# Block-decayed attention ahead of a mixture of experts: attention in blocks of 64 tokens instead of chunks of 128

## The chip, the cores and the metric

The kernel runs on one core of a Trainium2 chip. Of its engines, TensorE (PE in the profile) multiplies matrices: a weight load (PEld) puts up to 128 x 128 numbers into its array, then a matmul streams the other operand through it. A float32 matmul runs as two passes, so each appears twice in the counts. The array can be used in parts: a profile row that says 64\*64 worked on a quarter of it, 64\*128 on half of its rows, 128\*64 on half of its columns. VectorE (DVE), ScalarE (ACT) and GpSimd (POOL) work on tiles of 128 partitions; matmul results land in PSUM banks of 128 partitions x 512 floats. Sixteen DMA engines move data, started here almost only from SyncE's queue (SPq).

The metric is the device time of one execution in microseconds (us), the median of several.

## The reference

Attention over 4 batches, 8 heads, 768 tokens and 64 dimensions per head, in blocks of 64 tokens, with a decay `lam` per head; its output becomes `x`, 3072 tokens by 512, of a mixture of four experts.

```python
for b in range(nb):                                    # 12 blocks of 64 tokens
    qb, kb, vb = (q[:, :, sl], k[:, :, sl], v[:, :, sl])
    intra = np.einsum('bhic,bhjc->bhij', qb, kb) * Dmask[None]      # lam ** (i - j) for i >= j
    intra = np.einsum('bhij,bhjd->bhid', intra, vb)
    inter = np.einsum('bhid,bhde->bhie', qb * lam_pow[None], kv_state)   # lam ** (i + 1)
    out[:, :, sl] = intra + inter
    kb_dec = kb * rev_pow[None]                        # lam ** (63 - j)
    kv_state = lam_block * kv_state + np.einsum('bhsd,bhse->bhde', kb_dec, vb)   # lam ** 64
...
p = domain_probs / (domain_probs.sum(-1, keepdims=True) + 1e-09)
for e in range(4):
    h = np.maximum(x @ w1[e], 0.0)                     # 3072x512 by 512x1024
    out += p[:, e:e + 1] * (h @ w2[e])                 # 3072x1024 by 1024x512
```

Everything is float32. The block length isn't part of the result: any chunk length gives the same sums, with decays to match.

## The kernel before, in words

**Tiles.** Attention goes in 24 chunks of C = 128 tokens (6 of each batch, NCH), each with all 8 heads. Eight chunks (CPG) make a group of 1024 tokens, whose attention output, transposed, is `xT`, the operand of that group's expert products. There are three groups (g) and four experts (e). The expert products are Strassen products: seven half-size products M1 to M7 for x @ w1, each split into seven again (`first_product`, line 843, operands `xs_in` and `ws_in` prepared in DRAM and brought in by `feed`, two buffers each), and seven for h @ w2 (`second_product`, line 897, operand `w2t`). The last group uses a nested form for the second (line 1123), the first unit a direct form (line 1253).

**A chunk of attention** has three steps. Heads are kept in pairs: partitions 0 to 63 of `qT` and `kT` hold heads 0 to 3, partitions 64 to 127 heads 4 to 7 (`half[r]`).

- `turn` (line 520) transposes q and k on TensorE (line 529), copies them out of PSUM on ScalarE, scales q by its decays on VectorE (`qs`), and has GpSimd scale k in place by its decays (`decayed`). For chunks 2 to 5 of batches 2 and 3 q and k come rearranged through DRAM instead (`across`), and VectorE transposes them in 32 x 32 squares.
- `scores` (line 543) multiplies k by q for the whole chunk: per head 128 keys by 128 queries over 64 dimensions, 8 matmuls on half of the array's rows (line 551). VectorE multiplies them with the mask of decays, two operations of 512 elements (`mask`, line 95), into the tiles `st`.
- `values` (line 563) sums in the same PSUM banks the product with the state `kv` (line 574, 8 matmuls on quarters of the array, left out in a batch's first chunk) and that of `st` with v (line 579, 8 matmuls on half of its columns). In the second bank's free half it computes the products of decayed k and v for the state (line 587, 8 matmuls; left out in a batch's last chunk). ScalarE copies the sums to `xT`. VectorE then scales the state by lam ** 128 and adds the products (line 95; in a batch's first chunk a copy, line 599).

**Order.** The schedule is manual: each engine runs its instructions in the order in which the program issues them, and an instruction waits for its operands with everything behind it. Group 0's attention is a loop of ten slots: slot i holds turn(i), scores(i - 1), values(i - 2), in slot 3 scores ahead of turn; direct products stand between them from slot 4 on. Groups 1 and 2 have their attention as a list of 24 `steps` each, one or two of which are popped per Strassen product, so chunks 8 to 23 stand among the products of the group before. VectorE's share of such a step isn't issued at once: `soon` puts it at the head of a list, `background`, of which `rest` issues one entry per part of a product; for chunks 0 to 7 it is issued at once. Sums for the operands (GpSimd) and their stores are `chores`, which `pump` issues at a pace, from an account of GpSimd's work (`busy`).

q, k and v of chunks 0 to 3 are loaded ahead of the loop in the order q k of 0, q k of 1, v of 0, q k of 2, v of 1, q k of 3, a weight block, v of 2, v of 3; later chunks some slots ahead. Small tiles of 128 x 512 come from one pool of NPOOL = 47 buffers that is handed round in order.

**Tables.** `s_decay` (the mask, 8 scans over 128 elements) and `q_decay` (powers of lam by seven doublings) are computed on VectorE at the start, once `lam` has arrived; chunk 0's masks come behind them.

Of the kernel before, what the change touches and what calls it, by code (L numbers as in the profile page):

```python
# [14 lines left out]
FP32 = mybir.dt.float32  # L15
PSUM = bass.MemoryType.PSUM
DRAM = bass.MemoryType.DRAM
NPOOL = 47
AHEAD = 2


# [1 line left out]
def kernel(  # L23
# [30 lines left out]
    nc = tc.nc  # L54
# [3 lines left out]
    NTOK, DOUT = out.shape  # L58
    P = nc.NUM_PARTITIONS
    C = P  # L60
    NHP = H // 2
    NCH = S // C
    CPG = 8
# [76 lines left out]
    def store(f):  # L140
        queue.append((busy[0] + 2, f))

    def pump(pace=1.0, force=False):
        while results:
            results.pop(0)()
        while late and (force or late[0][0] <= now[0]):
            late.pop(0)[1]()
        begins = chores and (force or free[0] <= now[0])
        while queue and (force or queue[0][0] <= now[0] or begins and len(queue) > LEFT):
            queue.pop(0)[1]()  # L150
        if begins:
# [266 lines left out]

    s_decay = consts.tile([P, 2, NHP, C], FP32, name="s_decay")
    for r in range(2):
        for ac in range(NHP):
            h = 4 * r + ac
            nc.vector.tensor_tensor_scan(
                out=s_decay[:, r, ac], data0=lam_bc[:, h:h + 1].to_broadcast([P, C]), data1=ident[:],
                initial=0.0, op0=ALU.mult, op1=ALU.add,
            )

    k_decay = s_decay[:, :, :, C - 1]  # L430


    q_decay = consts.tile([P, NHP, C], FP32, name="q_decay")
    for r in range(2):
        nc.vector.tensor_copy(out=q_decay[half[r], :, 0], in_=lam_bc[half[r], 4 * r:4 * r + 4])
    m = 1
    while m < C:
        nc.vector.tensor_tensor(
            out=q_decay[:, :, m:2 * m], in0=q_decay[:, :, 0:m],
            in1=q_decay[:, :, m - 1:m].to_broadcast([P, NHP, m]), op=ALU.mult,  # L440
        )
        m *= 2

    kv = consts.tile([P, NHP, D], FP32, name="kv")

    probs = consts.tile([P, NTOK // P, E], FP32, name="probs")
    gate = consts.tile([P, NTOK // P, E], FP32, name="gate")
# [49 lines left out]
        if n < CPG:  # L497
            rest(len(work))

    def decayed(kn):  # L500

        kd = kn.rearrange("p (ac r) d -> p ac r d", r=2)
        by = k_decay.rearrange("p r ac -> p ac r").unsqueeze(3)
        tt(nc.gpsimd, kd, kd, by.to_broadcast([P, NHP, 2, D]), ALU.mult)

    def turn_across(n):

        qT, kT, kn = nat.pop((n, "qx")), nat.pop((n, "kx")), nat[n, "k"]
        qs = small("qs") if n % NCH else None

        def scaled():
            if n % NCH:
                tt(nc.vector, qs[:], qT[:], q_decay[:].rearrange("p h c -> p (h c)"), ALU.mult)
            turned[n] = qT, kT, qs

        soon(n, *(lambda x=x: nc.vector.transpose(out=x[:], in_=x[:]) for x in (qT, kT)), scaled)
        if n % NCH < NCH - 1:
            decayed(kn)

    def turn(n, tags):  # L520
        if comes_across(n):
            turn_across(n)
            return
        qn, kn = nat.pop((n, "q")), nat[n, "k"]
        qp = bank(tags[0], "qp")
        kp = bank(tags[1], "kp")
        for x, y in ((qp, qn), (kp, kn)):
            for ac in range(NHP):
# [4 lines left out]
        qT, kT, qs = small("qT"), small("kT"), None  # L533
        nc.scalar.copy(out=qT[:], in_=qp[:])
        nc.scalar.copy(out=kT[:], in_=kp[:])
        if n % NCH:
            qs = small("qs")
            soon(n, lambda: tt(nc.vector, qs[:], qT[:], q_decay[:].rearrange("p h c -> p (h c)"), ALU.mult))
        turned[n] = qT, kT, qs
        if n % NCH < NCH - 1:  # L540
            decayed(kn)

    def scores(n, tags):
        while n not in turned:
            rest(force=True)
        qT, kT, _ = turned[n]

        sp = [bank(tags[r], "sp") for r in range(2)]
        for ac in range(NHP):
            for r in range(2):  # L550
                nc.tensor.matmul(  # L551
                    out=sp[r][:, ac * C:(ac + 1) * C], lhsT=hc(kT)[half[r], ac], rhs=hc(qT)[half[r], ac],
                    start=True, stop=True,
                )
        st = [small("st") for _ in range(2)]

        def mask(hd):
            tt(nc.vector, st[hd][:], sp[hd][:], s_decay[:, hd].rearrange("p h c -> p (h c)"), ALU.mult)

        soon(n, *(lambda hd=hd: mask(hd) for hd in range(2)))  # L560
        masked[n] = st

    def values(n, tags):
        kn, vn = nat.pop((n, "k")), nat.pop((n, "v"))
        qs = turned.pop(n)[2]
        st = masked.pop(n)
        c = n % CPG
        first, last = n % NCH == 0, n % NCH == NCH - 1

        op = [bank(tags[r], "op") for r in range(2)]  # L570
        heads = [(a, r, c) for a in range(2) for r in range(2) for c in range(2)]
        if not first:
            for a, r, x in heads:
                nc.tensor.matmul(  # L574
                    out=op[r][half[x], a * C:(a + 1) * C], lhsT=kv[half[r], 2 * a + x], rhs=hc(qs)[half[r], 2 * a + x],
                    start=(a == 0), stop=False, skip_group_check=True,
                )
        for a, r, x in heads:
            nc.tensor.matmul(  # L579
                out=op[r][half[x], a * C:(a + 1) * C], lhsT=vn[:, 4 * r + 2 * a + x], rhs=hc(st[r])[:, 2 * a + x],  # L580
                start=(first and a == 0), stop=True, skip_group_check=True,
            )
        kvp = op[1][:, 2 * C:].rearrange("p (h d) -> p h d", d=D)
        if not last:
            for ac in range(NHP):
                for r in range(2):
                    nc.tensor.matmul(  # L587
                        out=kvp[half[r], ac], lhsT=kn[:, 2 * ac + r], rhs=vn[:, 4 * r + ac], start=(ac == 0), stop=True,
                        skip_group_check=True,
                    )  # L590
        for r in range(2):
            nc.scalar.copy(
                out=xT[:, 2 * r:2 * r + 2, c * C:(c + 1) * C],
                in_=op[r][:, 0:2 * C].rearrange("p (a t) -> p a t", t=C),
            )
        if not last:
            def state():
                if first:
                    nc.vector.tensor_copy(out=kv[:], in_=kvp)
                else:  # L600
                    tt(nc.vector, kv[:], kv[:], q_decay[:, :, C - 1:C].to_broadcast([P, NHP, D]), ALU.mult)
                    tt(nc.vector, kv[:], kv[:], kvp, ALU.add)

            soon(n, state)

    def attention(g):

# [2 lines left out]
        for n in range(g * CPG, (g + 1) * CPG):  # L610
# [3 lines left out]
            def end(n=n):  # L614
# [3 lines left out]
                values(n, ("s0", "s1"))  # L618
                if n + AHEAD < B * NCH:
                    load_more(n + AHEAD)  # L620
                if n == g * CPG + CPG // 2 - 1:
                    chores[0:0] = early
                if n == g * CPG + CPG - 1:
# [894 lines left out]
```

## Time and profile before

The median of three runs is 1185.82 us (1185.27 to 1186.21). One execution was profiled; its span, from the first to the last instruction, is 1183.3 us.

Busy time of the engines in four stretches, with the number of instructions; DMA is the mean busy share of the 16 DMA engines, the clock the granted TensorE clock as a share of full speed:

| us | what runs | PE busy | PE passes | DVE busy | ACT busy | POOL busy | clock | DMA |
|---|---|---|---|---|---|---|---|---|
| 0 to 57 | chunks 0 to 7, first direct products | 54.80 | 635 | 38.24 | 20.67 | 26.50 | 1.00 | 0.86 |
| 57 to 134 | direct products | 76.37 | 357 | 53.52 | 18.72 | 43.58 | 1.00 | 0.87 |
| 134 to 668 | products of groups 0 and 1, chunks 8 to 23 among them | 533.60 | 3192 | 359.85 | 94.54 | 247.29 | 1.00 | 0.93 |
| 668 to 1183.3 | products of the rest, no attention | 510.99 | 2380 | 339.05 | 140.08 | 311.36 | 1.00 | 0.72 |

Rows of attention, over the whole run:

| line, operands | what | passes or operations | median ns of one |
|---|---|---|---|
| 529 qp, kp | transposes of q and k (full array, 128 columns) | 128 | 273 |
| 551 sp<-qT,kT and the brought-across qx,kx | scores (half the rows, 128 columns) | 384 | 272 |
| 574 op<-qs,kv | with the state (quarters, 128 columns) | 320 | 269 |
| 579 op<-st,vn | with the values (half the columns, 128 columns) | 384 | 273 |
| 587 op<-vn,kn | products for the state (half the columns, 64 columns) | 320 | 222 |
| 95 st<-sp,s_decay (DVE) | masks, 128 x 512 | 48 | 680 |
| 95 kv<-op (DVE) | sum of the state, 128 x 256 | 16 | 421 |
| 95 kn<-kn,s_decay (POOL) | decays of k, 128 x 512 | 20 | 1060 |

The nanoseconds of one pass are its time from start to end. Passes follow each other before the one ahead has ended, so a row's time is not its count times this.

### The profile page before, as it was taken

What the parts mean: (1) busy time and instruction counts of PE and PEld (TensorE: products, weight loads), DVE (VectorE), ACT (ScalarE), POOL (GpSimd) and SP (SyncE); (2) the same over time, 40 slices, a digit from 0 to 9 for tenths busy, and PEclk for the clock granted to TensorE, in tenths of its full rate; (3) what the DMA queues carried; (4) which work ended last, traced back from release to release, by engine and by line L of the source; (5) the groups of instructions that cost most, each with busy time, mean ns of one, the idle gap of its engine ahead of it and who ended that gap; (6) DMA issues with size and microseconds to landing.
All of it is one profiled execution on the core that took longest, in us unless ns stands there. A gap on an engine that the chain in (4) does not pass through costs nothing.

```text
span 1183.3 us, 17880 instructions
## 1 busy us (share of the span) xinstructions
PE 1175.7 (99%) x6559; PEld 1022.7 (86%) x6559; DVE 790.7 (67%) x1333; ACT 274.0 (23%) x500; POOL 628.7 (53%) x600
## 2 busy tenths in 40 slices
PE   9999999999999999999999999999999999999998
PEld 8888888888888888888888888888888888888887
DVE  6785785567468857647856774773665676777785
ACT  3332122112211201211220120121243342341331
POOL 2756258349457900055244655416584693783884
PEclk9999999999999999999999999999999999999999
DMA  9797799999999997899998989998986657566543
GB/s 232 194 292 238 250 300 310 362 326 333 353 359 334 328 291 227 262 287 303 303 317 247 295 287 318 275 312 294 316 289 238 261 196 272 212 237 248 213 155 95
DMA packets 265608, 324.23 MB, mean 274 GB/s; under 512 B 121489, under 2 KB 206897, under 8 KB 265521
## 3 DMA queue, kind: packets, MB, share of 16 engines
q1 hardware_dynamic: 254912, 320.27, 81.6%
q10 hardware_dynamic: 10608, 2.82, 1.1%
q8 instruction: 52, 0.85, 0.3%
q14 instruction: 36, 0.29, 0.1%
HBM read 237.69 MB, written 89.54 MB: 277 GB/s over the span
## 4 chain that ended last, share of the span: by engine, by line
PE 94%; DVE 3%; DMA 2%; issue 0%; POOL 0%; SPq 0%; ACT 0%; DVEq 0%
PE pg L843 38%; PE q L897 32%; PE pq L1123 13%; PE pM L1253 2%; PE op L579 2%; PE sp L551 2%; PE pc L1253 2%; DMA w_ops<-ops 2%; PE op L574 1%; PE op L587 1%; DVE sums L95 0%; PE qp L529 0%; PE kp L529 0%; PE pg L1123 0%; DVE acc L95 0%; DVE m L95 0%
## 5 line engine op out<-in xcount | busy, mean ns | idle before, releaser
L843 PE MATMUL pg<-xs_in,ws_in 128*128 128x256 f32 x1960 | 469.8, 380 | 0.9 <-DVE m L95 0.9
L843 PEld LDWEIGHTS pg<-xs_in,ws_in 128*128 128x128 f32 x1960 | 371.2, 190 | 52.9 <-DVE m L95 2.3
L95 DVE TENSOR_TENSOR m<-pg,m 128x512 f32<-128x512 f32 x451 | 308.1, 687 | 106.5 <-PE pg L843 99.6
L897 PE MATMUL q<-w2t,hS 128*128 128x256 f32 x1024 | 243.4, 380 | 0.0
L897 PEld LDWEIGHTS q<-w2t,hS 128*128 128x128 f32 x1024 | 193.2, 190 | 27.0 <-issue 0.2
L913 DVE SCALAR_TENSOR_TENSOR acc<-q,gate,acc 128x256 f32<-128x256 f32 x192 | 92.5, 482 | 170.2 <-PE q L897 170.0
L897 PE MATMUL q<-w2t,m 128*128 128x256 f32 x768 | 182.7, 381 | 0.0
L897 PEld LDWEIGHTS q<-w2t,m 128*128 128x128 f32 x768 | 144.8, 190 | 20.5 <-issue 0.3
L855 ACT ACTIVATE m<-m 128x512 f32<-128x512 f32 x132 | 83.0, 630 | 283.6 <-DVE m L95 276.6
L95 POOL TENSOR_TENSOR m<-m,xT 128x512 f32<-128x512 f32 x64 | 80.7, 1276 | 71.6 <-ACT m L855 53.9
L95 POOL TENSOR_TENSOR kn<-kn,s_decay 128x512 f32<-128x512 f32 x20 | 22.5, 1126 | 140.7 <-PE kp L529 134.8
L95 DVE TENSOR_TENSOR sums<-pq,sums 128x256 f32<-128x256 f32 x153 | 64.2, 422 | 46.0 <-PE pq L1123 38.8
L851 ACT COPY m<-pg 128x512 f32<-128x512 f32 x88 | 51.6, 586 | 174.3 <-PE pg L843 173.4
L1123 PE MATMUL pq<-acc,w2t 128*128 128x256 f32 x352 | 86.6, 379 | 0.0
L95 POOL TENSOR_TENSOR ops<-w2b 128x256 f32<-128x256 f32 x24 | 17.9, 766 | 119.4 <-DMA w2b<-in_moe_w_dram 111.3
L1123 PEld LDWEIGHTS pq<-acc,w2t 128*128 128x128 f32 x352 | 66.8, 190 | 9.3 <-issue 0.3
L95 POOL TENSOR_TENSOR acc<-hT,hT 128x512 f32<-128x512 f32 x32 | 40.3, 1274 | 30.3 <-PE pq L1123 28.4
L95 POOL TENSOR_TENSOR w2o<-w2b 128x512 f32<-128x512 f32 x32 | 40.6, 1291 | 23.3 <-DMA w2b<-in_moe_w_dram 23.3
L786 ACT ACTIVATE m<-m 128x512 f32<-128x512 f32 x44 | 27.7, 630 | 101.8 <-DVE m L95 101.8
L95 DVE TENSOR_TENSOR hS<-m,m 128x512 f32<-128x512 f32 x56 | 45.3, 812 | 4.9 <-ACT m L855 4.9
L95 DVE TENSOR_TENSOR m<-m,m 128x512 f32<-128x512 f32 x56 | 47.2, 844 | 0.0
L95 POOL TENSOR_TENSOR acc<-hT,acc 128x512 f32<-128x512 f32 x32 | 40.7, 1273 | 7.4 <-PE pq L1123 5.4
(158 smaller groups left out, 1360.4 us busy)
## 6 DMA issues: line engine op xcount, KB each, us to landing
xs_in<-x_ops SPq DMA_DIRECT2D x70, 896.0 KB, 6.4
ws_in<-w_ops SPq DMA_DIRECT2D x70, 896.0 KB, 8.7
w2t<-w_ops SPq DMA_DIRECT2D x66, 256.0 KB, 6.8
w2t<-w_sums SPq DMA_DIRECT2D x64, 256.0 KB, 3.9
w_ops<-ops SPq DMA_DIRECT2D x28, 512.0 KB, 5.5
w2t<-in_moe_w_dram SPq DMA_DIRECT2D x48, 256.0 KB, 3.4
w2b<-in_moe_w_dram SPq DMA_DIRECT2D x32, 256.0 KB, 5.9
w_sums<-w2o SPq DMA_DIRECT2D x16, 512.0 KB, 5.1
```

The source lines that it names most:

```text
L95: eng.tensor_tensor(out=o, in0=a, in1=b, op=op)
L551: nc.tensor.matmul(out=sp[r][:, ac * C:(ac + 1) * C], lhsT=hc(kT)[half[r], ac], rhs=hc(qT)[half[r], ac], start=True, stop=True,)
L574: nc.tensor.matmul(out=op[r][half[x], a * C:(a + 1) * C], lhsT=kv[half[r], 2 * a + x], rhs=hc(qs)[half[r], 2 * a + x], start=(a == 0), sto ...
L579: nc.tensor.matmul(out=op[r][half[x], a * C:(a + 1) * C], lhsT=vn[:, 4 * r + 2 * a + x], rhs=hc(st[r])[:, 2 * a + x], start=(first and a = ...
L786: nc.scalar.activation(out=o[:], in_=o[:], func=AF.Relu)
L843: nc.tensor.matmul(out=p[:, j * 256:(j + 1) * 256], lhsT=ws[i][:, j * P:(j + 1) * P], rhs=xs[i], start=(fresh and j == 0), stop=True, skip ...
L851: nc.scalar.copy(out=new[at][:], in_=p[:])
L855: nc.scalar.activation(out=new[at][:], in_=new[at][:], func=AF.Relu)
L897: nc.tensor.matmul(out=p[:, s * DH:(s + 1) * DH], lhsT=h[A_OF[m]][:, c * 256 + s * P:c * 256 + (s + 1) * P], rhs=fed2[g, e, m][uu][:, c], ...
L913: nc.vector.scalar_tensor_tensor(out=o, in0=x, scalar=w, in1=o, op0=ALU.mult, op1=ALU.add)
L1123: nc.tensor.matmul(out=p[:, 0:256], lhsT=fed3[e, m, x // 2][:, x % 2, c * P:(c + 1) * P], rhs=b[B_OF[i]][:, c * 256:(c + 1) * 256], start= ...
L1253: nc.tensor.matmul(out=p[:, s * 256:(s + 1) * 256], lhsT=a[c][:, f:f + P], rhs=b[:, c, j * 256:(j + 1) * 256], start=(s == 0 and c == 0 an ...
```

## The change

Attention keeps its 24 chunks of 128 tokens and their steps, but treats each as two blocks of BL = 64 tokens (index x).

- `scores` multiplies keys and queries of the same block only: 16 matmuls of 64 x 64 by 64 columns, each on a quarter of the array (row half r, the heads; column half x, the block). The scores of both head halves fill 256 columns of a bank each, so the masks are two operations of 256 elements into one tile `st`.
- The products for the state move from `values` to `scores`, one set per block (16 matmuls of 64 x 64; 8 in a batch's last chunk), into the other 256 columns of the two banks. They read the decayed k, which is now a tile of its own (`kd`), made in `turn` for every chunk, and v.
- There are two states per chunk, one at the start of each block, in a tile that holds both. `middle` finishes the second (a sum on VectorE; a copy in a batch's first chunk), `end` makes the next chunk's: VectorE scales and adds, GpSimd scales the result once more by lam ** 64 (`passed`) as the base of the next chunk's second state. A batch's first state is cleared.
- `values` sums, per block, the products of q with that block's state and of `st` with that block's v: 16 + 16 matmuls of 64 x 64 by 64 columns, in every chunk. The array's row half is the heads for the first kind and the block for the second, so half of the first kind's sums, those with x != r, lie in the other bank; they go to columns of their own, and after ScalarE's copies to `xT` VectorE adds them to it (`adds`, issued by `all_added`, which `pump` and the steps call).
- The decay tables have half their length; the mask's scans start from a folded identity (`blk_ident`). The pool has 48 buffers.

```diff
-NPOOL = 47
+NPOOL = 48
...
+    adds = []
+
+    def all_added(still=None):
+        while adds and (still is None or adds[0][0] < still):
+            adds.pop(0)[1]()
+
     def pump(pace=1.0, force=False):
+        all_added(None if force else now[0])
...
-    s_decay = consts.tile([P, 2, NHP, C], FP32, name="s_decay")
+    blk_ident = small("bi")[:, 0:BL]
+    nc.vector.tensor_tensor(out=blk_ident, in0=ident[:, 0:BL], in1=ident[:, BL:C], op=ALU.add)
+    s_decay = consts.tile([P, 2, NHP, BL], FP32, name="s_decay")
     for r in range(2):
         for ac in range(NHP):
             h = 4 * r + ac
             nc.vector.tensor_tensor_scan(
...
-
-
-    q_decay = consts.tile([P, NHP, C], FP32, name="q_decay")
...
+
+    q_decay = consts.tile([P, NHP, BL], FP32, name="q_decay")
     for r in range(2):
...
             out=q_decay[:, :, m:2 * m], in0=q_decay[:, :, 0:m],
             in1=q_decay[:, :, m - 1:m].to_broadcast([P, NHP, m]), op=ALU.mult,
         )
         m *= 2
 
-    kv = consts.tile([P, NHP, D], FP32, name="kv")
+    states = {}
+
+    def by_block(t):
+        return t[:].rearrange("p (h x i) -> p h x i", x=2, i=BL)
+
+    def scale_q(qs, qT):
+        by = q_decay[:].unsqueeze(2).to_broadcast([P, NHP, 2, BL])
+        tt(nc.vector, by_block(qs), by_block(qT), by, ALU.mult)
+
+    def passed(eng, o, s):
+        tt(eng, o, s, q_decay[:, :, BL - 1:BL].to_broadcast([P, NHP, D]), ALU.mult)
 
...
-    def decayed(kn):
-
-        kd = kn.rearrange("p (ac r) d -> p ac r d", r=2)
-        by = k_decay.rearrange("p r ac -> p ac r").unsqueeze(3)
-        tt(nc.gpsimd, kd, kd, by.to_broadcast([P, NHP, 2, D]), ALU.mult)
+    def decayed(n):
+
+        kn = nat[n, "k"]
+        if comes_across(n):
+            kd = kn
+        else:
+            kd = small("kd")[:].rearrange("p (h d) -> p h d", d=D)
+        nat[n, "kd"] = kd
+        by = k_decay.rearrange("p r ac -> p ac r").unsqueeze(3).to_broadcast([P, NHP, 2, D])
+        tt(nc.gpsimd, *(x.rearrange("p (ac r) d -> p ac r d", r=2) for x in (kd, kn)), by, ALU.mult)
+
+    def begin_state(n):
+        if n % NCH == 0:
+            states[n] = small("kv")[:].rearrange("p (x h d) -> p x h d", x=2, d=D)
+            nc.vector.memset(states[n][:, 0], 0.0)
...
-        qT, kT, kn = nat.pop((n, "qx")), nat.pop((n, "kx")), nat[n, "k"]
-        qs = small("qs") if n % NCH else None
+        decayed(n)
+        del nat[n, "k"]
...
+        qs = small("qs")
...
-            if n % NCH:
-                tt(nc.vector, qs[:], qT[:], q_decay[:].rearrange("p h c -> p (h c)"), ALU.mult)
+            scale_q(qs, qT)
...
-        if n % NCH < NCH - 1:
-            decayed(kn)
...
     def turn(n, tags):
+        all_added()
+        begin_state(n)
         if comes_across(n):
...
-        qn, kn = nat.pop((n, "q")), nat[n, "k"]
+        decayed(n)
+        qn, kn = nat.pop((n, "q")), nat.pop((n, "k"))
...
+        qT, kT, qs = small("qT"), small("kT"), small("qs")
...
+        scaled = lambda: scale_q(qs, qT)
+        soon(n, scaled)
+        turned[n] = qT, kT, qs, scaled
...
     def scores(n, tags):
+        all_added()
         while n not in turned:
             rest(force=True)
-        qT, kT, _ = turned[n]
+        qT, kT = turned[n][0:2]
+        kd, vn = nat.pop((n, "kd")), nat[n, "v"]
+        first, last = n % NCH == 0, n % NCH == NCH - 1
 
         sp = [bank(tags[r], "sp") for r in range(2)]
+        blk = [slice(x * BL, (x + 1) * BL) for x in range(2)]
         for ac in range(NHP):
             for r in range(2):
...
+                for x in range(2):
+                    nc.tensor.matmul(
+                        out=sp[r][half[x], ac * BL:(ac + 1) * BL], lhsT=hc(kT)[half[r], ac, blk[x]],
+                        rhs=hc(qT)[half[r], ac, blk[x]], start=(ac == 0), stop=True, skip_group_check=True,
+                    )
+        for ac in range(NHP):
+            for x in range(1 if last else 2):
                 for r in range(2):
                     nc.tensor.matmul(
-                        out=kvp[half[r], ac], lhsT=kn[:, 2 * ac + r], rhs=vn[:, 4 * r + ac], start=(ac == 0), stop=True,
-                        skip_group_check=True,
+                        out=sp[x][half[r], 256 + ac * D:256 + (ac + 1) * D], lhsT=kd[half[x], 2 * ac + r],
+                        rhs=vn[half[x], 4 * r + ac], start=False, stop=True, skip_group_check=True,
                     )
+        st = small("st")
+        added = [sp[x][:, 256:512].rearrange("p (h d) -> p h d", d=D) for x in range(2)]
+
+        def mask(r):
+            tt(
+                nc.vector, st[:, r * 256:(r + 1) * 256], sp[r][:, 0:256], s_decay[:, r].rearrange("p h c -> p (h c)"),
+                ALU.mult,
+            )
+
+        def middle():
+            s = states[n][:, 1]
+            if first:
+                nc.vector.tensor_copy(out=s, in_=added[0])
+            else:
+                tt(nc.vector, s, s, added[0], ALU.add)
+
+        def end():
+            s = states[n + 1] = small("kv")[:].rearrange("p (x h d) -> p x h d", x=2, d=D)
+            passed(nc.vector, s[:, 0], states[n][:, 1])
+            tt(nc.vector, s[:, 0], s[:, 0], added[1], ALU.add)
+            passed(nc.gpsimd, s[:, 1], s[:, 0])
+
+        work = [lambda: (mask(0), mask(1)), middle] + ([] if last else [end])
+        soon(n, *work)
+        masked[n] = st, work
+
+    def values(n, tags):
+        all_added()
+        vn = nat.pop((n, "v"))
+        qs, *scaled = turned.pop(n)[2:]
+        st, work = masked.pop(n)
+        while any(f in background for f in (*scaled, *work)):
+            rest(force=True)
+        state = states.pop(n)
+        c = n % CPG
+
+        op = [bank(tags[x], "op") for x in range(2)]
+        cols = lambda a, r: slice((2 * r + a) * BL, (2 * r + a + 1) * BL)
+        apart = lambda a: slice((4 + a) * BL, (5 + a) * BL)
+
+        def inter(a, r, x, start):
+            for y in range(2):
+                nc.tensor.matmul(
+                    out=op[r][half[y], cols(a, r) if x == r else apart(a)], lhsT=state[half[r], x, 2 * a + y],
+                    rhs=by_block(qs)[half[r], 2 * a + y, x], start=start, stop=False, skip_group_check=True,
+                )
+
+        for a in range(2):
+            for r in range(2):
+                inter(a, r, 1 - r, a == 0)
+        for a in range(2):
+            for r in range(2):
+                inter(a, r, r, False)
         for r in range(2):
...
+            for a in range(2):
+                for x in range(2):
+                    for y in range(2):
+                        h = 2 * a + y
+                        nc.tensor.matmul(
+                            out=op[x][half[y], cols(a, r)], lhsT=vn[half[x], 4 * r + h],
+                            rhs=st[half[x], (4 * r + h) * BL:(4 * r + h + 1) * BL], start=False, stop=True,
+                            skip_group_check=True,
+                        )
+        for x in range(2):
+            o = xT[:, :, c * C + x * BL:c * C + (x + 1) * BL]
+            nc.scalar.copy(out=o, in_=op[x][:, 0:4 * BL].rearrange("p (a t) -> p a t", t=BL))
+            o = o[:, 2 * (1 - x):2 * (1 - x) + 2]
+            p = op[1 - x][:, 4 * BL:6 * BL].rearrange("p (a t) -> p a t", t=BL)
+            adds.append((now[0], lambda o=o, p=p: tt(nc.vector, o, o, p, ALU.add)))
 
     def attention(g):
 
...
                 values(n, ("s0", "s1"))
                 if n + AHEAD < B * NCH:
                     load_more(n + AHEAD)
+                if n % (CPG // 2) == CPG // 2 - 1:
+                    all_added()
                 if n == g * CPG + CPG // 2 - 1:
                     chores[0:0] = early
                 if n == g * CPG + CPG - 1:
...
 
     pairs = (("s0", "s1"), ("q01", "q02"), ("q11", "q12"))
     def x_sums(*halves):
+
+        all_added()
 
         for name, a, b in (("T1", "B12", "B11"), ("T2", "B22", "T1"), ("T3", "B22", "B12"), ("T4", "B21", "T2")):
             for i in range(2):

```

More of the change, by code (lines that the diff above doesn't have):

```diff
@@ L60 @@
     C = P
+    BL = C // 2
     NHP = H // 2
@@ L425 @@
             nc.vector.tensor_tensor_scan(
-                out=s_decay[:, r, ac], data0=lam_bc[:, h:h + 1].to_broadcast([P, C]), data1=ident[:],
+                out=s_decay[:, r, ac], data0=lam_bc[:, h:h + 1].to_broadcast([P, BL]), data1=blk_ident,
                 initial=0.0, op0=ALU.mult, op1=ALU.add,
             )
-    k_decay = s_decay[:, :, :, C - 1]
-    q_decay = consts.tile([P, NHP, C], FP32, name="q_decay")
+    k_decay = s_decay[:, :, :, BL - 1]
+    q_decay = consts.tile([P, NHP, BL], FP32, name="q_decay")
     for r in range(2):
@@ L436 @@
     m = 1
-    while m < C:
+    while m < BL:
         nc.vector.tensor_tensor(
@@ L498, in soon @@
             rest(len(work))
-    def decayed(kn):
-        kd = kn.rearrange("p (ac r) d -> p ac r d", r=2)
-        by = k_decay.rearrange("p r ac -> p ac r").unsqueeze(3)
-        tt(nc.gpsimd, kd, kd, by.to_broadcast([P, NHP, 2, D]), ALU.mult)
+    def decayed(n):
[11 more added lines that the diff above has]
+            nc.vector.memset(states[n][:, 0], 0.0)
     def turn_across(n):
-        qT, kT, kn = nat.pop((n, "qx")), nat.pop((n, "kx")), nat[n, "k"]
-        qs = small("qs") if n % NCH else None
+        decayed(n)
+        del nat[n, "k"]
+        qT, kT = nat.pop((n, "qx")), nat.pop((n, "kx"))
+        qs = small("qs")
         def scaled():
-            if n % NCH:
-                tt(nc.vector, qs[:], qT[:], q_decay[:].rearrange("p h c -> p (h c)"), ALU.mult)
+            scale_q(qs, qT)
             turned[n] = qT, kT, qs
         soon(n, *(lambda x=x: nc.vector.transpose(out=x[:], in_=x[:]) for x in (qT, kT)), scaled)
-        if n % NCH < NCH - 1:
-            decayed(kn)
     def turn(n, tags):
+        all_added()
+        begin_state(n)
         if comes_across(n):
@@ L532, in turn @@
                 )
-        qT, kT, qs = small("qT"), small("kT"), None
+        qT, kT, qs = small("qT"), small("kT"), small("qs")
         nc.scalar.copy(out=qT[:], in_=qp[:])
         nc.scalar.copy(out=kT[:], in_=kp[:])
[L536 to L541, printed above, removed]
+        scaled = lambda: scale_q(qs, qT)
@@ L543, in scores @@
+        soon(n, scaled)
+        turned[n] = qT, kT, qs, scaled
     def scores(n, tags):
+        all_added()
         while n not in turned:
             rest(force=True)
-        qT, kT, _ = turned[n]
+        qT, kT = turned[n][0:2]
+        kd, vn = nat.pop((n, "kd")), nat[n, "v"]
+        first, last = n % NCH == 0, n % NCH == NCH - 1
         sp = [bank(tags[r], "sp") for r in range(2)]
+        blk = [slice(x * BL, (x + 1) * BL) for x in range(2)]
         for ac in range(NHP):
             for r in range(2):
[L551 to L585, printed above, removed]
@@ L589, in values @@
-                        skip_group_check=True,
-                    )
-        for r in range(2):
[L592 to L604, printed above, removed]
+                        out=sp[x][half[r], 256 + ac * D:256 + (ac + 1) * D], lhsT=kd[half[x], 2 * ac + r],
```

## The prediction

> **What bounds the kernel now.** I read the page's busy times first, then its chain of waits, then the timeline of TensorE around one chunk of attention.
>
> ```profile
> PE 1175.7 (99%) x6559; PEld 1022.7 (86%) x6559; DVE 790.7 (67%) x1333; ACT 274.0 (23%) x500; POOL 628.7 (53%) x600
> ...
> PE 94%; DVE 3%; DMA 2%; issue 0%; POOL 0%; SPq 0%; ACT 0%; DVEq 0%
> ```
>
> TensorE is busy for 99% of the span and holds 94% of the chain, at a granted clock of 10 tenths in all slices. From 134 to 668 us, where chunks 8 to 23 of attention are spread among the products, it is busy for 533.6 of 534 us. So a microsecond taken from its queue there is a microsecond of the end, as long as nothing else is late. Chunk 8 looks like this (start, length, line, operands, count; a float32 matmul runs as two passes, so 8 matmuls are x16):
>
> ```profile
> 139.11 1.03 PE L843 MATMUL pg<-xT,w1b 128*128 128x256 f32 x4
> 140.07 1.16 PE L551 MATMUL sp<-qT,kT 64*128 64x128 f32 x16
> 141.16 1.99 PE L897 MATMUL q<-w2t,hS 128*128 128x256 f32 x8
> 142.99 1.03 PE L843 MATMUL pg<-xT,ops 128*128 128x256 f32 x4
> ...
> 153.35 1.03 PE L843 MATMUL pg<-xt,w1o 128*128 128x256 f32 x4
> 154.31 0.67 PE L574 MATMUL op<-qs,kv 64*64 64x128 f32 x16
> 154.91 1.09 PE L579 MATMUL op<-st,vn 128*64 128x128 f32 x16
> 155.83 0.63 PE L587 MATMUL op<-vn,kn 128*64 128x64 f32 x16
> 156.40 1.99 PE L897 MATMUL q<-w2t,m 128*128 128x256 f32 x8
> 158.23 1.03 PE L843 MATMUL pg<-xt,ops 128*128 128x256 f32 x4
> ```
>
> Full-array passes of 256 columns follow each other every 0.216 us (eight take 1.73 us in the chain). So the first L843 row's stream is over at 139.97, and the L897 row, undisturbed, would have begun at 142.99 - 1.73 = 141.26: the scores cost 1.29 us. In the same way the values stage costs 156.50 - 154.21 = 2.29 us. A chunk takes 3.58 us, its transposes apart.
>
> **The price of a small pass.** 128 columns should stream for half of 0.216, 0.108 us. L551 has 2 row tiles side by side: 8 steps of 0.108 = 0.87, leaving 0.42 us for going into another array shape and back. L587 is the nearest row to the new products: 64 columns, two column tiles. One pass lasts 0.222 us, the row 0.63, so 7 steps take 0.41: 0.058 us a step. L574 shows that four quarters run at once:
>
> ```profile
> L574 PE MATMUL op<-qs,kv x320: 269/269/320, 16.1 to 666.4; 64*64 64x128 f32 x160
> ```
>
> ```profile
> 154.31 0.34 PE L574 MATMUL op<-qs,kv 64*64 64x128 f32 x4
> 154.31 0.42 PEld L574 LDWEIGHTS op<-qs,kv 64*64 64x64 f32 x16 [0.33 <-issue]
> ```
>
> The first line is L574's passes over the run (fastest, median and slowest in ns), the others a narrow window of the timeline. The first four passes last at most 0.320 us each and together 0.34: they start some 7 ns apart. The 16 weight loads, 0.133 us each, start within 0.42 - 0.13 = 0.29 us, 19 ns apart at the most.
>
> **After, on TensorE.** Scores become 16 matmuls of 64 columns on four quarters, 32 passes; the state's products move from the values stage to stand behind them, 32 passes more (16 in a batch's last chunk). Values becomes 32 passes with the state and 32 with the values, all in one shape. Not shown anywhere: a long run of 64-column passes on four quarters. From below, four passes per step of 0.058 us, 14.5 ns each; from above, the rule weighed next. I take 14.5, for L587 and L574 are the same operation with one dimension changed each. Both new stages are then 16 steps x 0.058 + 0.42 = 1.35 us.
>
> - Middle chunk: scores 1.29 to 1.35 (0.06 worse), values 2.29 to 1.35 (0.94 better): 0.88 saved.
> - First of a batch: before, no L574 (0.60 in the chain): values 1.69 to 1.35, scores 0.06 worse: 0.28.
> - Last of a batch: before, no L587 (0.46 in the chain): values 1.83 to 1.35; scores 1.29 to 12 x 0.058 + 0.42 = 1.12: 0.65.
>
> There are 16 middle, 4 first and 4 last chunks: 14.1 + 1.1 + 2.6 = **17.8 us** if all of it counts. Chunks 8 to 23 (11, 2 and 3 of these) hold 9.7 + 0.6 + 1.9 = 12.2. TensorE should show 6559 - 1408 + 3008 = 8159 passes.
>
> **A rule against it.** The Trainium skill (TensorE: Matmul & The Clock Gate, "Wait — 56ns, not 53.3ns?") says that matmuls never start less than about 25 ns apart, however few columns they have. By it each stage is 64 x 0.025 + 0.42 = 2.02 us, a middle chunk 4.04 instead of 3.58, and the whole is slower: 16 x 0.46 + 4 x 1.06 + 4 x 0.52 = 13.7 us. The row contradicts it for different tiles, with 7 ns between starts, but only inside a group; averaged over a step, no row goes below 27 ns, because none has the work for it. The break-even is at about 21 ns. I go by the row, and keep the other end as a rival.
>
> **What stands in the way in the first stage (0 to 57 us).** There the chunks' loads arrive just in time (DMA share 0.86). The state's products need v in the scores stage, one slot earlier. v of chunk 2 is issued at 12.26 us and lands 4.8 later, at 17.1. Its scores started at 14.03; now they start about 13.9 (values of chunk 0 begin at 12.6, after VectorE's decays, and take 1.35), and their second half stands at 14.5 waiting for v to 17.1. Behind it in TensorE's queue are the transposes of chunk 3 (15.12 before) and all later work. They start at 17.1 + 0.46 + 0.2 = 17.8: 2.7 us late. After that, values of chunks 1 to 7 give 5 x 0.94 + 0.48 + 0.34 and scores take back 0.07: 5.45. Net 2.75. v of chunks 0 and 1 land at 8.6 and 11.6, when they are needed; k's decayed copy is done over 1.4 us before its use in every chunk. The decay tables are half as long: the last of VectorE's doubling steps (0.43) and part of the scans (2.63 for eight) go, but a copy of q's scaling (0.69), a clear and a fold of the identity come, so masks of chunk 0 end about when they did (12.7).
>
> **The helpers.** VectorE per middle chunk: two masks of 256 (0.42 each, by the row of the state's sum out of PSUM) for two of 512 (0.68), but a third state operation (0.42) and two sums into xT of 128 elements (about 0.29, from 0.68 and 0.42 by a line): 2.9 to 3.35 us, 11 us more of 790.7. It lies in VectorE's idle third, but at the ends of products VectorE is behind: TensorE waits 0.3 to 0.5 us there three times. I add 1 us. GpSimd gets four more decays (1.06) and 20 state scalings (about 0.73): 19 us, in its idle 47%; without that cover, the scaling is needed only by the next chunk, over 25 us later, and the decay by the scores, 3 us or more after it is done in the tightest chunk (12). The SP queue keeps its 979 instructions in their order.
>
> **DMA.** From 134 to 668 us its share is 0.93, and near 1.0 from 200 to 375. The weights for a product issued at 327.0 land at 336.6 and are used at 337.4; those of 400.8 land at 409.1 and are used at 410.0. With products up to 1 us shorter, some such transfers will be late; each late one costs TensorE a few tenths. I take 1.5 us, between 0 and 6 (half of the 12.2, if DMA sets the pace there).
>
> **Sum.** 12.2 + 2.75 - 1 - 1.5 = 12.5 us. The span is 1183.3; the median of 1185.82 has 2.5 us around it that don't change. Forecast **1173.3 us**.
>
> **Rivals.**
> - *All of it arrives* (chance 0.15): v isn't waited for, because later slack absorbs the wait, and no transfer is late. 1185.8 - 17.8 = 1168.0. For it: TensorE waits almost nowhere now. Against: the landing of v.
> - *DMA and VectorE eat most* (0.14): 6 us to late transfers and 3 to VectorE instead of 2.5 leave 6 us: 1179.8. For it: the share near 1.0. Against: SP itself waits for TensorE 28 us between 200 and 410, so the transfers have room to start earlier.
> - *Issue decides* (0.10): passes start 25 ns apart: 1185.8 + 13.7 = 1199.5. Slower from 21 ns on. For it: the rule, and that no row shows a mean below 27. Against: the 7 ns.
> - *Gain and loss cancel* (0.04), near 1186; some other loss, such as GpSimd standing on a transfer with a chunk's decay behind it (0.02), slower.
>
> The forecast itself has 0.55. Faster by over 0.2% (2.4 us, about what the measurement can tell from nothing): 0.15 + 0.55 + 0.14 = 0.84; within it 0.04; slower 0.12. The range reaches over the first rival, with 1.5 us to spare for decays that end earlier, and to the second with the same: 1166.5 to 1181.3.
>
> **What would show it.** A score row of x32 whose next row starts 0.5 us later, and 1.3 to 1.4 us from first pass to the next full-array row: the 14.5 ns. If the 32 passes take 0.8 us, issue decides. A wait of TensorE on v's transfer near 14 to 17 us, about 2.6 us: the first stage. Waits on xs_in or ws_in between 200 and 420 us: DMA. TensorE's busy time near 1161. The prediction is wrong if the new passes are not four abreast, or if TensorE waits for GpSimd's decayed k or scaled state.

## The result and the profile after

The changed kernel takes 1181.38 us (median of 5 runs, 1180.15 to 1183.66) against 1186.09 us in the runs beside it: ratio 0.9959, 95% interval 0.9947 to 0.9971. That is 4.7 us less where 12.5 were forecast, and just above the range. The profiled span went from 1183.3 to 1179.1 us.

The lines of the page that answer to the first ones shown of before:

```profile
PE 1159.9 (98%) x8159; PEld 1011.2 (86%) x8159; DVE 793.6 (67%) x1417; ACT 272.5 (23%) x500; POOL 651.0 (55%) x624
...
PE 95%; DVE 3%; DMA 1%; SPq 1%; issue 0%; ACT 0%; ACTq 0%; DVEq 0%
```

TensorE has exactly the 8159 passes that were counted and is busy for 15.8 us less. But the span fell by 4.2 only: 11.6 us came back as idle time. The answer on TensorE's waits names nearly all of it (what waited, for what; us in total, times, longest):

```profile
PE op L638 <- DVE kv L96: 3.9, 3, 1.3
PE sp L592 <- DMA vn<-in_v_dram: 3.1, 1, 3.1
PE qp L561 <- issue: 1.7, 1, 1.7
PE pM L1315 <- ACT xT L661: 1.3, 1, 1.3
PE pM L1315 <- DVE xT L96: 1.3, 1, 1.3
...
PE op L654 <- issue: 0.9, 1, 0.9
PE pM L1315 <- DVE xt L96: 0.6, 1, 0.6
```

To see where each came from, I compared the start of every full-array matmul of the products (4952 passes, in one order in both kernels) in the two traces. The changed kernel is 6.5 us late at the first direct product, 3.7 us late at 57 us of before and 4.56 us late at 62, where the product behind the last chunk of the first stage has waited for that chunk's sums. Then it gains, with one relapse, to 4.94 us early:

| what is passed (us of before) | moves by, us |
|---|---|
| first stage, to 62 (3.70 of it by 57) | +4.56 |
| values of chunks 8 to 10, 16, 19 to 22 (middle) | -0.99 each |
| values of chunks 13, 14, 15 (middle; at 320, 349, 379) | +0.63 each |
| values of chunks 12, 18 (first of a batch) | -0.40 each |
| values of chunks 11, 17, 23 (last of a batch) | -0.53 each |
| scores of any chunk from 8 on | within 0.04 |
| ends of products where TensorE had waited for VectorE (131, 384 and others) | -1.0 in all |

**The price of the new passes** is what L574 and L587 promised. Chunk 19's values in the timeline (start, length, line, operands, count):

```profile
540.77 1.89 PE L959 MATMUL q<-w2t,hS 128*128 128x256 f32 x8
542.59 0.69 PE L638 MATMUL op<-qs,kv 64*64 64x64 f32 x32
543.11 0.65 PE L654 MATMUL op<-st,vn 64*64 64x64 f32 x32
543.68 1.99 PE L905 MATMUL pg<-xs_in,ws_in 128*128 128x256 f32 x8
545.51 0.81 PE L959 MATMUL q<-w2t,hS 128*128 128x256 f32 x3
```

32 passes take 0.46 to 0.52 us, 14.5 to 16 ns each. The product ahead has streamed for 1.73 us at 542.50, the next begins at 543.68: the stage costs 1.18 us, or 1.28 up to where that next product would have begun undisturbed, which is how the prediction read its stages (the row behind it starts at 545.51, less 1.73). The Trainium skill's limit of 25 ns between starts (TensorE: Matmul & The Clock Gate, "Wait — 56ns, not 53.3ns?") does not hold for four quarters together: by it the 64 passes alone would last 1.6 us. The same stage before:

```profile
541.05 1.89 PE L897 MATMUL q<-w2t,hS 128*128 128x256 f32 x8
...
544.95 1.99 PE L843 MATMUL pg<-xs_in,ws_in 128*128 128x256 f32 x8
546.78 1.46 PE L897 MATMUL q<-w2t,hS 128*128 128x256 f32 x6
```

It cost 541.05 + 1.73 to 544.95, 2.17 us, or 2.27 in the prediction's way. Either way the change saves 0.99 us.

**The three chunks that lose** show their wait in two windows of the timeline, TensorE's and VectorE's, at chunk 13:

```profile
318.37 0.33 PE L638 MATMUL op<-qs,kv 64*64 64x64 f32 x4
320.01 0.62 PE L638 MATMUL op<-qs,kv 64*64 64x64 f32 x26 [1.31 <-DVE kv L96]
```

```profile
317.62 0.69 DVE L96 TENSOR_TENSOR m<-pg,m 128x512 f32<-128x512 f32 x1
318.48 0.69 DVE L96 TENSOR_TENSOR m<-pg,m 128x512 f32<-128x512 f32 x1 [0.17 <-PE pg L905]
319.09 0.41 DVE L96 TENSOR_TENSOR kv<-kv,q_decay 128x256 f32<-128x256 f32 x1
319.54 0.42 DVE L96 TENSOR_TENSOR kv<-kv,sp 128x256 f32<-128x256 f32 x1
```

Four passes run (they write the first bank), then TensorE waits until the last VectorE row has ended at 319.96. That row, the entry `end`, makes the state of the next chunk, which values(13) does not read. But it reads the state's products from the second bank of `sp`, and `op[1]` of values takes the same PSUM bank ("s1"). In these chunks only three parts of products lie between scores and values, `background` gives out one entry per part, and the third entry comes just ahead of values, behind two sums of products.

**The first stage** around the wait for v of chunk 2, on TensorE:

```profile
14.31 0.62 PE L654 MATMUL op<-st,vn 64*64 64x64 f32 x27 [0.91 <-issue]
...
14.79 0.68 PE L585 MATMUL sp<-qT,kT 64*64 64x64 f32 x29
18.53 1.13 PE L592 MATMUL sp<-vn,kd 64*64 64x64 f32 x32 [3.07 <-DMA vn<-in_v_dram]
19.59 1.11 PE L561 MATMUL qp<-ident,qn 128*128 128x128 f32 x4
20.50 1.06 PE L561 MATMUL kp<-ident,kn 128*128 128x128 f32 x4
21.49 1.13 PE L638 MATMUL op<-qs,kv 64*64 64x64 f32 x32
22.40 1.03 PE L654 MATMUL op<-st,vn 64*64 64x64 f32 x32
24.74 1.96 PE L1315 MATMUL pM<-xT,w1b 128*128 128x256 f32 x8 [1.31 <-ACT xT L661]
```

The passes after the wait take twice as long as elsewhere (L592 to the next row 1.06 us, elsewhere 0.46). The windows say why; the third number from the right is the granted clock:

```profile
14.70:18.50 3.80, 0.76 (x51) 0.62 (x39) 1.15 (x4) 0.65 (x2) 0.62 (x1) 0.73 0.92 230
18.50:24.70 6.20, 4.89 (x104) 4.34 (x104) 3.02 (x8) 1.82 (x4) 2.94 (x3) 0.62 0.80 204
```

In the trace's clock records the clock is half from 16.42 to 23.25 us. Five rows of attention then take 4.9 us instead of about 2.5.

### The profile page after: what moved, and what is told of

The parts are those of the page before. It is cut to its first block, busy times and chain, and to the rows that moved or that the text cites. A ratio compares the mean times of both kernels' runs of the same rounds, so it can differ in the third digit from the quotient of the medians.

```text
span 1179.1 us, 21213 instructions
## 1 busy us (share of the span) xinstructions
PE 1159.9 (98%) x8159; PEld 1011.2 (86%) x8159; DVE 793.6 (67%) x1417; ACT 272.5 (23%) x500; POOL 651.0 (55%) x624
## 3 DMA queue, kind: packets, MB, share of 16 engines
q8 instruction: 65, 1.06, 0.4%
## 4 chain that ended last, share of the span: by engine, by line
PE 95%; DVE 3%; DMA 1%; SPq 1%; issue 0%; ACT 0%; ACTq 0%; DVEq 0%
PE pg L905 39%; PE q L959 33%; PE pq L1185 13%; PE pM L1315 2%; PE pc L1315 2%; PE op L638 1%; PE sp L585 1%; PE op L654 1%; DVE m L96 1%; PE sp L592 1%; PE qp L561 1%; PE kp L561 1%; DVE sums L96 0%; DMA vn<-in_v_dram 0%; DVE hS L96 0%; SPq L124 0%
## 5 line engine op out<-in xcount | busy, mean ns | idle before, releaser
L96 POOL TENSOR_TENSOR kv<-kv,q_decay 128x256 f32<-128x256 f32 x20 | 13.9, 696 | 161.9 <-DVE kv L96 132.9
```

What stands on the lines that cost most here:

```text
L96: eng.tensor_tensor(out=o, in0=a, in1=b, op=op)
```

## The experiments

The ten kernels below are all derived from the changed one; "after" is the changed kernel at 1181.4 us. Times are medians, ratios stand against the kernel before.

**1 (e1). State products of chunk 2 put off.**

```diff
-        for ac in range(NHP):            # products for the state, in scores
+        def products():
...
+        if n != 2:
+            products()
...
+            if i == 3 and lag == 2:      # behind the values of chunk 1
+                put_off.pop()()          # products of chunk 2, then middle and end
```

> The changed kernel with one part of the change undone for one chunk: the state's products of chunk 2 go behind the values of chunk 1 instead of behind the scores of chunk 2. Theory A (the first stage lost its gain because TensorE stood for v of chunk 2 from 15.4 to 18.5 us, which also halved its granted clock from 16.4 to 23.3 us): the wait falls from 3.07 us to under 1, the granted clock stays at 1.0, and so the passes from 18.5 to 23.3 us run twice as fast (some 2 us) and the products stand between the values of chunk 1 and the first direct product, which hides most of its 1.31 us for ScalarE's copies: 5 to 6 us less than the changed kernel, 1175.5 to 1176.5. Theory B (the first stage is set by DMA whatever TensorE does, so the wait only moves to a later load): less than 2 us, 1179.5 to 1181.5.

Measured: 1181.09 us, ratio 0.9961 (0.9946 to 0.9976): nothing gained. Yet the wait for v is gone, the clock is 1.00 up to 47 us, and the first direct product starts at 21.7 instead of 24.7 us. TensorE's timeline shows what took the place:

```profile
18.91 0.34 PE L664 MATMUL op<-st,vn 64*64 64x64 f32 x5 [1.10 <-issue]
19.03 0.69 PE L595 MATMUL sp<-vn,kd 64*64 64x64 f32 x32
21.72 1.97 PE L1325 MATMUL pM<-xT,w1b 128*128 128x256 f32 x8 [2.00 <-issue]
...
27.57 0.52 PE L648 MATMUL op<-qs,kv 64*64 64x64 f32 x21 [1.80 <-issue]
...
47.97 1.09 PE L561 MATMUL qp<-ident,qn 128*128 128x128 f32 x4 [2.84 <-issue]
```

The last of these holes brings the halved clock back: by the clock records it is half from 47.45 to 50.87 us, and the rows from 47.97 on last longer for it (some 1.4 us in all, half of the time to 50.87). Theory A is right about the wait and the clock behind it and wrong about the gain. B is wrong too, for the profile shows no load of data at the end of any of these holes. They are of two kinds, which runs 4 and 5 tell apart.

**2 (e2). v of chunk 2 loaded sooner.**

```diff
+    load(2, "v")
     raw_w1(0, "A11")
-    load(2, "v")
```

> The changed kernel with the load of v of chunk 2 issued ahead of the first weight block (two transfers of 256 KB) instead of behind it. Theory A (TensorE's wait for v and the halved clock behind it): v lands some 2 us sooner, at 16 to 16.5 us; the wait falls to about 1 us[...]; 3.5 to 5 us less than the changed kernel, 1176.5 to 1178. Theory B (DMA sets the stage): the weight block lands later by the same and the first direct product waits for it instead: less than 2 us.

Measured: 1181.19 us, 0.9957 (0.9944 to 0.9970). v lands at 15.6, the wait is 0.7 us, the clock does not fall behind it, and the first direct product starts 3.8 us sooner. By 51 us nearly all of this is lost again: to holes without a releaser (the longest before 27 us 1.4 us, another of 2.0 us at 44 to 46), and to the clock, which is half from 47.29 to 50.70 us while TensorE has passes all the time (some 1.7 us, half of that stretch).

**3 (e3). State entries with the masks.**

```diff
-        work = [lambda: (mask(0), mask(1)), middle] + ([] if last else [end])
+        work = [lambda: (mask(0), mask(1), middle())] + ([] if last else [end])
```

> The changed kernel with VectorE's three entries per chunk (masks; state of the second block; state of the next chunk) made into two: the second is issued with the masks. Theory A (in chunks 13, 14 and 15 the third entry is issued only just ahead of the values stage, and values cannot write its second PSUM bank until that entry has read the state's products from it): the three waits of 1.31 us at 318, 348 and 379 us go, and with them 3 x 1.6 = 4.9 us: 1176 to 1177; each of these chunks then gains 1.0 us against the kernel before, as chunks 8, 9 and 10 do. Theory B (VectorE is simply late there, whatever the order of its entries, because it has 0.4 us more to do per chunk): the waits stay or move to the products' own sums, less than 1.5 us.

Measured: 1179.04 us, 0.9935 (0.9917 to 0.9954). Of the three waits 0.2 us is left, and chunks 13 to 15 move by -0.74, -1.00 and -0.45 instead of +0.63 each; `end` is over at 318.5 us where it was 320.0. Theory A holds for the mechanism. Of the 4.9 us only 1.6 reach the end (by the traces; 2.3 by the medians), for now TensorE is ahead of the kernel before from 320 us on, and a new wait appears:

```profile
PE pg L905 <- DMA ws_in<-w_ops: 1.6, 2, 1.1
```

It lies at 337.7 and 410.0 us, the two places that the prediction had named as tight. Against the kernel before, TensorE loses 0.7 and 1.4 us there, and 0.2 at each of two more places.

**4 (e4). TensorE's code shifted by 64 instructions.**

```diff
-    warm(10)
+    warm(6)
+    p = bank("g3", "zp")
+    for _ in range(20):
+        nc.tensor.matmul(out=p[0:D, 0:D], lhsT=zeros[0:D, 0:D], rhs=zeros[0:D, 0:D], start=True, stop=True)
```

> The changed kernel with 64 more instructions on TensorE ahead of the first transposes (4 of the 10 warming matmuls replaced by 20 small ones), nothing else. Theory C (the two holes in TensorE's queue at 13.4 to 14.3 and 46.1 to 47.8 us, which no semaphore ends, are waits for the next block of code: they stand after 449 and 1675 of the trace's TensorE records): the holes begin after the same number of records, so 16 matmuls earlier in the program, or go where that place falls into another wait. Rival (they wait for something that the profile does not name, at a fixed place of the program): they stay in front of the same matmuls. The time is within 1.5 us of the changed kernel.

Measured: 1183.02 us (one run), 1.6 more than after; in this run the clock was half for 10.24 us (17.59 to 27.83) instead of 6.83. The hole after 449 records is gone; a new one of 0.7 us stands after 1985 records, in the middle of the values of chunk 5. The hole at 47 us stayed in front of the same matmul, now after 1739 records. So the two holes of the changed kernel were of two kinds, which the expectation had taken for one: the first is code, the second is not.

In all profiles together the holes of the first kind lie after 449, 705, 961, 1729, 1985 or 2241 records of TensorE (matmuls, weight loads, semaphores), always 449 plus a multiple of 256, whatever instruction stands there. This fits code that comes by DMA in blocks: the page counts 65 transfers of 16 KB in one instruction queue for 16587 records of TensorE, before 52 for 13367, about one per 256, so I take that queue for TensorE's.

```profile
q8 instruction: 65, 1.06, 0.4%
```

The Trainium skill (Runtime: NRT & Kernel Launch, "Instruction fetch mechanics") has the same blocks of 256 and calls the cost of their crossing mostly hidden. In the traces each hole of this kind ends 1.2 to 1.5 us after a transfer of that queue has ended. While blocks hold mostly passes of 256 columns, no such hole shows. A block of 64-column passes alone is used up in 128 x 14.5 ns = 1.9 us (an estimate: half of the records are weight loads), while the transfers of data keep the DMA engines at 0.8 to 1.07 up to 41 us. In run 1 TensorE went on past record 705 at 18.91; the next code transfer began at 25.31 and ended at 26.28, and TensorE, out of code at 25.8, went on at 27.57. Why a code transfer begins so late is not shown; that it queues behind the data is my guess.

**5 (e5). Sums into xT sooner.**

```diff
                 f(n, pairs[n % 3])
+            if lag == 2:
+                all_added()
```

> The changed kernel with VectorE's two sums into xT issued right behind each chunk's values in the first stage, instead of one step later, where they stand behind the sums of a direct product. Theory D (these sums are on TensorE's path there: the product at 39.3 us waits 1.27 us for those of chunk 3, the transposes at 47.8 us wait 1.69 us for the PSUM bank that those of chunk 4 still read, the product at 62.1 us waits 0.55 us for those of chunk 7): the second and third wait go and the first falls to about 0.4 us: 2.5 to 3 us less than the changed kernel, 1178.4 to 1178.9. Rival (VectorE now stands for ScalarE's copies with the next masks behind it, and TensorE waits for these): less than 1 us.

Measured: 1178.78 us, 0.9938 (0.9923 to 0.9953), 2.6 us less than after: theory D. The second kind of hole is VectorE's new sums. In the changed kernel those of chunk 4 stood behind two sums for x's operands, and chunk 7's transposes needed the bank that they read:

```profile
46.42 0.88 DVE L96 TENSOR_TENSOR acc<-xT,acc 128x256 f32<-128x256 f32 x2
...
47.23 0.48 DVE L96 TENSOR_TENSOR xT<-xT,op 128x128 f32<-128x128 f32 x2
...
47.81 0.63 PE L561 MATMUL qp<-ident,qn 128*128 128x128 f32 x4 [1.69 <-issue]
```

The sums end at 47.71, the transposes begin at 47.81. With the edit they begin without waiting, and of holes without a releaser only 0.6 us is left up to 57 us, at record 1729.

**6 (e6). No sums into xT.**

```diff
-            adds.append((now[0], lambda o=o, p=p: tt(nc.vector, o, o, p, ALU.add)))
```

> The changed kernel without VectorE's two sums into xT per chunk, so that half of the products of q with the state never reach xT and the output is not the reference's. Theory D (the sums cost TensorE 1.31 us at 24.7, 1.27 at 39.3, 1.69 at 47.8 and 0.55 us at 62.1): together 4.0 to 4.8 us less, span 1174.3 to 1175.1. Rival (only the copies ahead of the sums matter at 24.7 us, and code that comes late fills what is freed): 2 to 3 us less, span 1176 to 1177.

Measured: 1178.95 us (one run), span 1177.1, 2.0 less than after. This is the rival's size, and what the rival named is there: all waits for the sums are gone, but at the first product 0.7 us of the 1.31 is left for ScalarE's copies, code is late by 0.4 and 0.6 us (records 1729 and 2241), and the wait for v is 4.7 us instead of 3.1. More comes from the clock: behind the longer wait it is half for 10.24 us (18.48 to 28.72), and TensorE is busy for 8.86 of them, where the changed kernel had 6.83 and 4.72. Half of the difference of 4.14, some 2.1 us by this estimate, went there, so the run does not refute the 4 us of theory D.

**7 and 8 (e7, e8). Three remedies together.** Run 7 has the edits of 2, 3 and 5, run 8 those of 1, 3 and 5 (for chunk 2 the entries stay apart).

> Three edits together: v of chunk 2 ahead of the first weight block, the sums into xT right behind values, the state's entries issued with the masks. If they add: e2 alone reached the first direct product 3.8 us sooner than the changed kernel and lost 3.7 of it again, 1.7 at the transposes of chunk 7 (the sums of theory D, which go here) and 2.1 to code that was late at records 705 and 961 (which stays); so 1.7 + 3 (sums) + 1.6 to 2.3 (state, as e3) = 6 to 7 us less than the changed kernel: 1174.5 to 1175.5. If code sets the pace of the first stage once the other waits are gone: 1176.5 to 1178.

> As the run before, but with the products of chunk 2 behind the values of chunk 1 instead of v loaded sooner; the sums of chunk 1 now come ahead of the state's entries of chunk 2 on VectorE, which took 2.0 us before the first direct product in e1. If they add: 1174 to 1175.5. If code sets the pace: 1176.5 to 1178, with the holes again after 449 + 256 k records of TensorE.

Measured: run 7 1177.89 us (1174.04 to 1180.1), 0.9928 (0.9906 to 0.9950), with 2.4 us of waits for ws_in in its profile; run 8 1174.46 us (1172.48 to 1175.99), 0.9897 (0.9881 to 0.9914). In run 8 the effects add, though code is late after records 705 and 961 (a hole after record 2241 the profile puts down to VectorE) and the clock is half from 28.04 to 31.45 us. The longest hole is

```profile
26.58 0.52 PE L651 MATMUL op<-qs,kv 64*64 64x64 f32 x21 [2.33 <-issue]
```

**9 and 10 (e9, e10). Blocks for chunks 8 to 23 only.** Chunks 0 to 7 run `turn`, `scores` and `values` of the kernel before.

```diff
-        order = [(turn, 0), (scores, 1), (values, 2)]
+        order = [(turn_0, 0), (scores_0, 1), (values_0, 2)]    # chunks of 128
...
+    def block_tables():                                         # short tables out of the long ones
+        for x in range(2):
+            nc.scalar.copy(out=s_decay[half[x]], in_=s_all[half[x], :, :, x * BL:(x + 1) * BL])
...
+                if n == CPG - 1:                                # state of chunk 7 handed over as a pair
+                    s = states[CPG] = small("kv")[:].rearrange("p (x h d) -> p x h d", x=2, d=D)
+                    nc.vector.tensor_copy(out=s[:, 0], in_=kv[:])
+                    passed(nc.gpsimd, s[:, 1], s[:, 0])
```

> The change for chunks 8 to 23 alone: chunks 0 to 7 as in the kernel before (chunks of 128, state products behind the values, one state), with the long decay tables; two copies on ScalarE cut the short ones out of them, and the state of chunk 8 is handed over as a pair. Theory A + C + D together (the first stage is the only place that the change made slower, by v, late code and the sums into xT, 4.6 us): the first stage takes what it took before, within 0.5 us, and chunks 8 to 23 gain the 9.5 us that they gained in the changed kernel, three waits of 1.31 us included: 1176.3 to 1177.0, some 4.7 us less than the changed kernel. Rival (the loss of the first stage only moves: its code is still late when the blocks begin, or VectorE's and ScalarE's added work delays the direct products): 1178 to 1181.

> As the run before, with the state's entries on VectorE issued with the masks. If transfers were not in the way: 4.9 us less than that, 1171.5. In the other kernels with this edit the operands of the products at 337 and 410 us came late as soon as TensorE was 1 us or more ahead of the kernel before, and took 0 to 3.3 us back: 1172 to 1175 is expected. If more than 3.3 us is lost to ws_in, DMA sets the pace of this stage: above 1175.

Measured: run 9 1176.45 us, 0.9919 (0.9903 to 0.9936), as theory A + C + D had it: at 57 us it is 0.2 us behind the kernel before, from 62 us on it is not behind, no hole without a releaser is left, and the clock is 1.00 throughout. Of its waits the longest are the three of the bank:

```profile
PE op L644 <- DVE kv L96: 3.9, 3, 1.3
PE zp L421 <- DVE xT L416: 1.1, 1, 1.1
```

Run 10, with the state's entries sooner, takes **1172.67 us, 0.9892 (0.9877 to 0.9907)**, the fastest of all, 13.2 us under the kernel before. In its profile the wait for ws_in is 0.6 us, and of its lead over the kernel before TensorE gives back 1.3 us between 350 and 455 us.

## Why the prediction was wrong

- **The price of a pass: right.** 14.5 ns were taken, 14.5 to 16 came. Read in the prediction's way, a new stage is 1.28 us instead of 1.35, so its fixed part is 0.35, not 0.42; the stages of before were 1.28 and 2.27, as read off. A middle chunk saves 0.99 us (forecast 0.88), a first 0.40 (0.28), a last 0.53 (0.65). In a last chunk the 16 passes for the state use only two of the quarters, and took as long as 32 on four (0.56 and 0.57 us from the row's start to the next row's, at 245.63 and 216.28 us): eight more steps, where the forecast had four. For chunks 8 to 23 all this makes 13.3 us where 12.2 were forecast.
- **"Net 2.75" for the first stage: this step failed.** It was -4.56. The gain was there: by the chunk prices above, 5 x 0.99 + 2 x 0.40 + 0.53 = 6.3 us (forecast 5.45, without chunk 0). The wait for v was named at the right place, and it was 3.07 us; the forecast had 2.7 for all of its effect. v landed at 18.4, not 17.1, because it was issued 1.1 us later and took 5.1 us. What was not in the sum: the halved clock behind that wait (some 2.4 us, half of the 4.72 busy us in the halved stretch); VectorE's sums into xT (1.31 + 1.27 + 1.69 + 0.55, of which 0.7 at the first product belongs to ScalarE's copies, by run 6); late code (0.91). Together 11.2 - 6.3 = 4.9, near the 4.56.
- **Two covers were overlooked there.** Before, the state's products stood between the values and the first direct product and hid ScalarE's copies; the change moved them away. And the sums were costed by VectorE's idle third, though in this stage the next product reads xT at once, and VectorE works in order, behind sums that wait for TensorE.
- **The helpers, "I add 1 us": this step failed too, in kind.** The waits at the ends of products fell by 1.0 us. But the third state operation cost 3 x 1.62 = 4.9 us by holding a PSUM bank. The text had asked whether TensorE waits for decayed k or the scaled state; neither was late. That the state's products had moved into the banks of the scores, which values use next, was in the diff and not thought through.
- **DMA, 1.5 us: nothing in the changed kernel, right as a limit.** It was behind the kernel before until 514 us, so its transfers had their time. As soon as runs 3, 7, 8 and 10 went ahead, late starts of products between 249 and 455 us cost them 2.6, 4.1, 1.1 and 1.3 us against the kernel before, of which the waits name ws_in for 1.6, 2.4, 0 and 0.6; the rest is not named. With the measured terms the forecast's sum is 13.3 - 4.56 + 1.0 - 4.9 = 4.8 us, and the last product was 4.94 us early.
- **The rival "DMA and VectorE eat most"** had nearly the measured time, 1179.8, but by luck, not by its cause; most was lost in the first stage, and to VectorE through a bank. The rival "issue decides" is refuted as a pass price; code that arrives late is another limit, and shows in the first stage only.

## What to carry to other kernels

When a step that writes PSUM is moved, follow the bank, not only the data: whoever reads it last now stands ahead of the next user of the bank, in the order of the slowest queue. Look for what the moved work had been hiding, first of all copies that the next instruction needs. And a form that does the same work in more, smaller instructions can be worth it among long products and a loss at a start where everything arrives just in time: price the two places apart, and change only the one that pays, as run 10 does.

## What the runs showed of the hardware

- Small passes on four quarters of the array start 14.5 ns apart on the average, with a weight load for each: 32 in 0.46 us. On two quarters they start twice as far apart.
- TensorE can stand still where no semaphore is waited for: holes of 0.3 to 2.3 us after record 449 plus a multiple of 256, each ending 1.2 to 1.5 us after a 16 KB code transfer, where blocks were used up in a few us beside busy DMA engines.
- In the changed kernel the granted clock was halved for 6.83 us (16.42 to 23.25) when TensorE had been without a pass for 1.0 us; another hole of 0.9 us had ended 2.1 us before. A wait of 3 us so cost nearly twice its length. In all nine profiles with blocks in the first stage (after, runs 1 to 8) the clock was half somewhere in it, for 3.41, 6.83 or 10.24 us, and in the three with chunks of 128 there (before, runs 9 and 10) never. What exactly makes it fall is not shown: in run 2 it fell while passes ran, 1.3 us after a hole of 2.0 us.
